# A Fourier layer and a squared-ReLU MoE on one core: a second buffer for the MoE's sums, their cast moved by a block, a fixed order of the MoE's instructions

## The chip, the core and the metric

One core of a Trainium2 chip runs the whole program. The metric is the device time of one execution in microseconds; the number given for a kernel is the median of its runs. Beside the times there is a profile of one execution, taken by the hardware profiler. In it PE is TensorE (matmuls), PEld its weight loads, DVE is VectorE, ACT ScalarE, POOL GpSimd and SP the engine that issues most DMAs. L473 is line 473 of the kernel.

## What is computed

```python
def _attn_ref(x, w_r, w_i, b_r, b_i):
    X = np.fft.rfft(x, axis=1)
    Yr = Xr @ w_r - Xi @ w_i + b_r
    Yi = Xr @ w_i + Xi @ w_r + b_i
    Yr = np.sign(Yr) * np.maximum(np.abs(Yr) - 0.01, 0.0)   # and Yi
    y = np.fft.irfft(Y, n=x.shape[1], axis=1)

def _moe_ref(x, w_in, w_out):                # 24064 x 256, 256 x 2048, 2048 x 256
    h = x @ w_in
    r = np.maximum(h, 0.0)
    return (r * r) @ w_out
```

Eight sequences of 3008 rows go through a real Fourier transform, a complex 256 x 256 mix with a bias, a soft threshold and the inverse transform. The 24,064 rows that come out go through a two-layer network of width 2048 with a squared ReLU.

## The kernel before

**Numbers in two parts.** A value in float32 is split into a high part (a cast to fp32r, on ScalarE) and a low part (value minus high part, on VectorE or GpSimd). A product takes three matmuls: high by high, low weight by high, high weight by low. The helper `halves` (L164) makes the two parts; its copy is at L89 (ScalarE) or L90 (VectorE), its subtraction at L93. These helper lines are shared by many steps, so the profile's groups are told apart by the tile that they write.

**Transforms.** The first sequence is transformed in a phase of its own (`Fwd32`, `Unit32`), together with the preparation of all weights. For the other sequences, small units of work (`Fwd`, `Pair`, `Back`) run beside the MoE of the sequence before. `Pair.load_back` (L268) loads the matrix `kcm` with a DMA that GpSimd issues. The transforms use the two PSUM banks `psf`.

**The MoE.** A sequence is cut into 6 tiles of 504 or 500 rows, so there are 48 tiles in all. Two halves of a tile's rows (`h` is 252 or 250) and two blocks of 128 hidden units make a 2 x 2 block matrix, which is multiplied with the 2 x 2 blocks of `w_out` by a scheme of seven products in place of eight (Strassen-Winograd). A *step* takes two such blocks of hidden units; a tile has 8 steps, the program 384. A step `n` consists of:

- `block(0)` and `block(1)` (L464): six matmuls each into one of two PSUM banks `psh` (L473), contraction over 256. For block 0, ScalarE writes relu to `mr` (L480) and VectorE multiplies it with max(psh, 0) into the first half of `mc` (L481). For block 1, ScalarE writes relu into the second half of `mc` (L483) and squares it in place (L484). `mc` has two buffers.
- raw parts: at the end of `block(1)`, three of the four quarters of `mc` are split into high and low parts `mb`, in two pieces, one of `h` columns and one of `2h` (L490, L491).
- sums: GpSimd makes the four sums `ms` in three instructions, one of `2h` columns (L493) and two of `h` (L494, and L495 by way of L93). `ms` has one buffer.
- `split` (L497): the four sums are split into high and low parts `mt`, `4h` columns (1008 or 1000), a ScalarE cast and a VectorE subtraction.
- `out(0)` and `out(1)` (L500): nine matmuls with the raw parts and twelve with the sums (L515), into four PSUM banks `pso` that accumulate over the tile's 8 steps. After the last step `drain` (L524) copies the banks into `me`, GpSimd makes six additions (L539), and two DMAs store the tile.

**What sets the order.** The main loop (L645) goes in half steps, `m` = 2n + k. In program order a half step holds `block(k)` of step n, at k = 0 the `split` of step n - 1, then `out(k)` of step n - 2, and then those transform jobs that are due. This order is a priority only: a planner in the compiler, which plays the program through with modelled times, puts each engine's instructions in a fixed order, and takes what it thinks ready first. `tc.issue_after` ties an instruction behind another on the same engine; before, only the first matmuls into a shared bank are tied that way. Each engine then works its list in order and waits wherever an instruction's data or buffer is not ready. Numbers of buffers stand in `MAIN` (L39); a tile not named there has two.

Of the kernel before, what the change touches and what calls it, by code (L numbers as in the profile page):

```python
# [9 lines left out]
F32 = mybir.dt.float32  # L10
# [29 lines left out]
    "xs": 1, "xe": 1, "kv": 1, "kp": 1, "kq": 1, "ksh": 1, "ksl": 1, "kxl": 1, "kb": 1, "mr": 1, "ms": 1, "me": 1,  # L40
# [10 lines left out]

A11, A12, A22, S1, S2, S3, S4 = range(7)
B11, B21, B22 = range(3)
# [4 lines left out]
def fnet_moe(ctx: ExitStack, tc, x, w_r, w_i, b_r, b_i, w_in, w_out, bm, cm, dx, a32, c32, out):  # L58
    nc = tc.nc
    act, dve, pool = nc.scalar, nc.vector, nc.gpsimd  # L60
# [31 lines left out]
    def sub(eng, out, a, b):  # L92
        return eng.tensor_tensor(out=out, in0=a, in1=b, op=ALU.subtract)  # L93
# [70 lines left out]
    def halves(hi, lo, v, eng):  # L164
        copy(act, hi, v)
        sub(eng, lo, v, hi)
# [21 lines left out]
    def wout_sums(n, pair):  # L188
        w = pair[0].wide
        a = w.rearrange("p n (f i d) -> p n f i d", f=2, i=2)  # L190
        a11, a21, a12, a22 = (a[:, :, f, i] for f in range(2) for i in range(2))
        st = T("ds", [128, 2, 4, 128], F32)
        s1, s2, s3, s4 = (st[:, :, j] for j in range(4))
        dve.tensor_add(out=s1, in0=a21, in1=a22)
        sub(dve, s2, s1, a11)
        sub(dve, s3, a11, a21)
        sub(dve, s4, a12, s2)
        hi, lo = (v[:, n:n + 2] for v in wout)
        halves(hi[:, :, A11], lo[:, :, A11], a11, dve)
        halves(hi[:, :, A12:A22 + 1], lo[:, :, A12:A22 + 1], a[:, :, 1], dve)  # L200
        halves(hi[:, :, S1:], lo[:, :, S1:], st, dve)
# [213 lines left out]
    yts = {}  # L415
# [42 lines left out]
    acc, begun = {}, {}  # L458

    class Step:  # L460
# [3 lines left out]
        def block(self, j):  # L464
# [6 lines left out]
            for c in range(2):  # L471
                for k, y in ((0, yh), (1, yh), (0, yl)):
                    nc.tensor.matmul(ps, win[k][:, c, fs], y[:, c, :w], start=n == 0, stop=n == 5)  # L473
                    n += 1
            if j == 0:
                self.c = T("mc", [128, 4 * HM], F32)[:, :2 * w]
            c = self.c[:, j * w:(j + 1) * w]
            if j == 0:
                r = T("mr", [128, 2 * HM], F32)[:, :w]
                act.activation(r, ps, AF.Relu)  # L480
                dve.scalar_tensor_tensor(out=c, in0=ps, scalar=0.0, in1=r, op0=ALU.max, op1=ALU.mult)  # L481
                return
            act.activation(c, ps, AF.Relu)  # L483
            act.activation(c, c, AF.Square)  # L484
# [8 lines left out]
            pool.tensor_tensor(out=s[:, T1:T3 + 1], in0=c[:, 1::2], in1=c[:, 0:2], op=ALU.subtract)  # L493
            pool.tensor_tensor(out=s[:, T2], in0=c[:, 0], in1=s[:, T3], op=ALU.add)  # L494
            sub(pool, s[:, T4], c[:, 2], s[:, T2])  # L495

        def split(self):  # L497
            halves(self.sum[0], self.sum[1], self.s, dve)

        def out(self, j):  # L500
            t, n, h = self.t, self.n, self.h
            if n == j == 0:
# [4 lines left out]
                ((A12, self.raw, B21, o[0], 0), (S4, self.raw, B22, o[0], 1), (A11, self.raw, B11, o[1], 0)),  # L507
# [3 lines left out]
            for a, g, b, ps, i in products:  # L511
                for k, (w, v) in enumerate(((0, 0), (1, 0), (0, 1))):
                    first = n == k == 0
                    with tc.issue_after(begun[id(ps)].ins) if first and i else nullcontext():
                        mm = nc.tensor.matmul(  # L515
                            ps[:, i], wout[w][:, n, a], g[v][:, b], start=first and i == 0,
                            stop=n == NF // 2 - 1 and k == 2 and (i == 1 or a == A22),
                        )
                    if first and not i:
                        begun[id(ps)] = mm  # L520
# [3 lines left out]
        def drain(self, j):  # L524
# [8 lines left out]
            copy(act, e[:, 4:6], o[1])  # L533
            copy(act, e[:, 6:8], o[2])
            copy(dve, e[:, 2], o[3][:, 0])
            p2, c22, p1, u2, p5, p7 = (e[:, k] for k in (0, 3, 4, 5, 6, 7))

            def add(out, a, b):
                pool.tensor_tensor(out=out, in0=a, in1=b, op=ALU.add)  # L539
# [7 lines left out]
            b, c0, _ = tiles[t]  # L547
            for d in range(2):
                nc.sync.dma_start(
                    out[b, :, d, c0:c0 + 2 * h], e[:, 2 * d:2 * d + 2].rearrange("p j h -> p (j h)")  # L550
                )
            del acc[t], yts[t]
# [91 lines left out]
    jobs = []  # L644
    for m in range(2 * len(steps) + 6):  # L645
# [111 lines left out]
```

## Time and profile before

| what | value |
|---|---|
| median of 3 runs | 2942.83 us (2940.08 to 2944.81) |
| the profiled execution's own time | 2942.48 us |
| its span, first to last instruction | 2940.7 us |
| mean granted TensorE clock | 0.966 |
| DMA, mean over the span | 85 GB/s |

The span is what the profile's rows add up to; the profiled execution takes about 2 us more than it. Busy shares are averages over the first phase, the long middle and an end with few transforms, so the prediction reads stretches apart. In the groups of instructions the columns are: line, engine, operation, output tile and input tiles, partitions x elements, count, then busy us and mean ns of one, then the engine's idle time just before them and what ended it. A row of the timeline has start, length, engine, line, operation, tiles, form, how many instructions were merged, and in brackets the idle time before and who ended it.

### The profile page before, as it was taken

The page shows a single profiled execution, that of the slowest core. Times are in us where ns is not written, and L with a number is a line of the kernel's source. Part 1 is how long each engine was busy: PE and PEld are TensorE (multiplying, and loading weights), DVE is VectorE, ACT ScalarE, POOL GpSimd, SP SyncE. Part 2 cuts the span into 40 slices and gives each one's busy share as a digit, 9 for nine tenths or more (in the row PEclk, how much of TensorE's full clock was granted, in tenths as well). Part 3 has the DMA queues.
Part 4 walks back from the last instruction along what each step waited for, and adds up shares of the span by engine and source line. Part 5 has one row for each costly group of instructions (what it writes and reads, how often), then busy time and mean ns, then how long its engine had stood idle before and what let it go on. Part 6 is the DMA issues. An engine that isn't in the chain of part 4 may idle for free.

```text
span 2940.7 us, 47049 instructions
## 1 busy us (share of the span) xinstructions
PE 2685.1 (91%) x16856; PEld 2406.9 (82%) x16856; DVE 2081.2 (71%) x3035; ACT 1789.2 (61%) x3562; POOL 2012.1 (68%) x2082
## 2 busy tenths in 40 slices
PE   5699999999999999999999999999999999998987
PEld 4588888888888898888878888888878888888877
DVE  5857876788668776678757777577775777766654
ACT  3466666666666666666656666665656665666654
POOL 3367768777776678766686667766677667666665
PEclk8899999999999999999999999999999999999998
DMA  8442324223323223322232222322233222110000
GB/s 245 154 115 87 100 82 120 84 90 97 94 80 90 78 84 106 96 81 78 63 115 84 78 83 82 104 74 80 82 92 99 72 78 85 56 35 31 24 15 15
DMA packets 191260, 250.47 MB, mean 85 GB/s; under 512 B 21755, under 2 KB 135667, under 8 KB 191027
## 3 DMA queue, kind: packets, MB, share of 16 engines
q1 hardware_dynamic: 178627, 224.85, 24.8%
q0 software_dynamic: 12400, 22.61, 3.4%
q8 instruction: 134, 2.20, 0.3%
q14 instruction: 99, 0.81, 0.1%
HBM read 146.85 MB, written 100.53 MB: 84 GB/s over the span
## 4 chain that ended last, share of the span: by engine, by line
POOL 34%; PE 30%; DVE 15%; issue 8%; ACT 7%; DMA 1%; SPq 0%; POOLq 0%; DVEq 0%; ACTq 0%
PE psh L473 14%; PE pso L515 10%; POOL ms L493 9%; POOL me L539 7%; DVE mt L93 6%; POOL ms L494 6%; POOL ms L93 6%; ACT mt L89 4%; PE psf L300 3%; POOL xs L232 3%; DVE kv L321 2%; DVE mb L93 2%; POOL ksl L93 2%; DVE mc L481 1%; POOL yt L93 1%
## 5 line engine op out<-in xcount | busy, mean ns | idle before, releaser
L473 PE MATMUL psh<-yt,win 128*128 128x500 f32 (+1 forms) x4608 | 1239.9, 404 | 93.6 <-DVE mc L481 91.8
L473 PEld LDWEIGHTS psh<-yt,win 128*128 128x128 f32 x4608 | 838.2, 194 | 246.7 <-DVE mc L481 117.8
L493 POOL TENSOR_TENSOR ms<-mc 128x500 f32<-128x500 f32 (+1 forms) x384 | 502.0, 1307 | 559.8 <-DVE mt L93 557.1
L93 DVE TENSOR_TENSOR mb<-mc,mb 128x500 fp32r<-128x500 f32 (+3 forms) x768 | 697.7, 918 | 136.2 <-ACT mb L89 132.9
L515 PEld LDWEIGHTS pso<-mt,wout 128*128 128x128 f32 x4608 | 653.6, 193 | 64.4 <-ACT mt L89 10.5
L515 PE MATMUL pso<-mt,wout 128*128 128x250 f32 (+1 forms) x4608 | 686.2, 285 | 9.9 <-ACT mt L89 8.4
L89 ACT CAST mt<-ms 128x1000 fp32r<-128x1000 f32 (+1 forms) x384 | 395.9, 1031 | 475.2 <-POOL ms L93 474.0
L93 DVE TENSOR_TENSOR mt<-ms,mt 128x1000 fp32r<-128x1000 f32 (+1 forms) x384 | 494.8, 1289 | 109.7 <-ACT mt L89 106.8
L515 PE MATMUL pso<-mb,wout 128*128 128x250 f32 (+1 forms) x3456 | 537.4, 284 | 21.2 <-DVE mb L93 21.1
L481 DVE SCALAR_TENSOR_TENSOR mc<-psh,mr 128x500 f32<-128x500 f32 (+1 forms) x384 | 260.5, 678 | 387.5 <-POOL ms L93 368.6
L515 PEld LDWEIGHTS pso<-mb,wout 128*128 128x128 f32 x3456 | 466.2, 189 | 35.1 <-DVE mb L93 26.1
L89 ACT CAST mb<-mc 128x500 fp32r<-128x500 f32 (+3 forms) x768 | 386.5, 508 | 21.4 <-DVE mc L481 8.7
L93 POOL TENSOR_TENSOR ms<-mc,ms 128x250 f32<-128x250 f32 (+1 forms) x384 | 314.4, 819 | 21.3
L494 POOL TENSOR_TENSOR ms<-mc,ms 128x250 f32<-128x250 f32 (+1 forms) x384 | 307.8, 802 | 22.0
L480 ACT ACTIVATE mr<-psh 128x500 f32<-128x500 f32 (+1 forms) x384 | 227.1, 591 | 136.0 <-PE psh L473 133.3
L539 POOL TENSOR_TENSOR me<-me 128x250 f32<-128x250 f32 (+3 forms) x288 | 288.1, 1018 | 30.0 <-ACT me L89 23.3
L484 ACT ACTIVATE mc<-mc 128x500 f32<-128x500 f32 (+1 forms) x384 | 242.1, 630 | 1.2
L483 ACT ACTIVATE mc<-psh 128x500 f32<-128x500 f32 (+1 forms) x384 | 224.5, 585 | 10.7 <-PE psh L473 10.4
L300 PE MATMUL psf<-wx,kxh 128*128 128x256 f32 x1008 | 209.4, 285 | 11.0 <-DVE kul L93 8.7
L93 POOL TENSOR_TENSOR yt<-dy,yt 128x376 fp32r<-128x376 f32 (+3 forms) x168 | 153.1, 917 | 51.2 <-ACT yt L89 46.6
L232 POOL TENSOR_TENSOR xs<-xt 120x256 f32<-120x256 f32 x182 | 164.6, 925 | 24.7 <-PE psf L235 18.1
L300 PEld LDWEIGHTS psf<-wx,kxh 128*128 128x128 f32 x1008 | 167.2, 190 | 16.2 <-DVE kul L93 12.8
(91 smaller groups left out, 2914.2 us busy)
## 6 DMA issues: line engine op xcount, KB each, us to landing
du<-s SPq DMA_DIRECT2D x128, 256.0 KB, 3.0
s<-kuh SPq DMA_DIRECT2D x192, 128.0 KB, 2.0
s<-kul SPq DMA_DIRECT2D x192, 128.0 KB, 2.5
s<-xe SPq DMA_DIRECT2D x92, 240.0 KB, 2.4
xt<-x_in SPq DMA_DIRECT2D x91, 240.0 KB, 3.1
kcm<-cm_in POOLq DMA_DIRECT2D x84, 256.0 KB, 3.5
ka<-s SPq DMA_DIRECT2D x84, 256.0 KB, 3.2
du<-s SPq DMA_DIRECT2D x256, 64.0 KB, 3.0
```

What stands on the lines that cost most here:

```text
L89: return act.copy(out=out, in_=in_)
L93: return eng.tensor_tensor(out=out, in0=a, in1=b, op=ALU.subtract)
L232: pool.tensor_tensor(out=u[:, t], in0=self.xt[:, 0, 0], in1=self.xt[:, 0, 1], op=(ALU.add, ALU.subtract)[t])
L300: self.last = nc.tensor.matmul(ps, l, wx[j][:, k, c, :], start=n == 0, stop=n == 5)
L473: nc.tensor.matmul(ps, win[k][:, c, fs], y[:, c, :w], start=n == 0, stop=n == 5)
L480: act.activation(r, ps, AF.Relu)
L481: dve.scalar_tensor_tensor(out=c, in0=ps, scalar=0.0, in1=r, op0=ALU.max, op1=ALU.mult)
L484: act.activation(c, c, AF.Square)
L493: pool.tensor_tensor(out=s[:, T1:T3 + 1], in0=c[:, 1::2], in1=c[:, 0:2], op=ALU.subtract)
L494: pool.tensor_tensor(out=s[:, T2], in0=c[:, 0], in1=s[:, T3], op=ALU.add)
L515: mm = nc.tensor.matmul(ps[:, i], wout[w][:, n, a], g[v][:, b], start=first and i == 0, stop=n == NF // 2 - 1 and k == 2 and (i == 1 or a ...
L539: pool.tensor_tensor(out=out, in0=a, in1=b, op=ALU.add)
```

## The change

- `ms` gets a second buffer. `mr` goes: the relu of block 0 is written into `mc` itself, and L481's product works in place there. `kcm` has one buffer instead of two.
- A helper `then` ties each MoE instruction behind the last one given to it on the same engine. It covers the matmuls of `block` and `out`, the relu, product and square, the three GpSimd sums, and the casts and subtractions of `mb` and `mt`. The drain's copies and additions are not tied.
- The order of a half step becomes `out(k)` of step n - 2, `block(k)` of step n, then at k = 1 the split of the sums of step n - 1 and the split of the raw parts of step n. So the cast of the sums stands behind the second block of the next step, no longer ahead of it.
- The roles of the two row halves are exchanged, so that the three raw quarters lie side by side and are split in one piece of `3h` columns (756 or 750). One sum (S3 of the weights, T3 of the activations) changes its sign, and places in `me` and the order of two products change.
- The drain's six additions and the store are taken out of `drain` into `finish`, and done one by one, one each half step, over the next seven half steps.

The core of the diff:

```diff
-    "xs": 1, "xe": 1, "kv": 1, "kp": 1, "kq": 1, "ksh": 1, "ksl": 1, "kxl": 1, "kb": 1, "mr": 1, "ms": 1, "me": 1,
+    "xs": 1, "xe": 1, "kv": 1, "kp": 1, "kq": 1, "ksh": 1, "ksl": 1, "kxl": 1, "kb": 1, "kcm": 1, "me": 1,
-B11, B21, B22 = range(3)
+B11, B22, B21 = range(3)
-        sub(dve, s3, a11, a21)
+        sub(dve, s3, a21, a11)
+    acc, last_of = {}, {}
+    def then(eng, op, *args, **kwargs):
+        with tc.issue_after(last_of[eng].ins) if eng in last_of else nullcontext():
+            last_of[eng] = op(*args, **kwargs)
+    def then_halves(hi, lo, v):
+        then(act, copy, act, hi, v)
+        then(dve, sub, dve, lo, v, hi)
...
-                    nc.tensor.matmul(ps, win[k][:, c, fs], y[:, c, :w], start=n == 0, stop=n == 5)
+                    then(pe, pe.matmul, ps, win[k][:, c, fs], y[:, c, :w], start=n == 0, stop=n == 5)
+            then(act, act.activation, c, ps, AF.Relu)
             if j == 0:
-                r = T("mr", [128, 2 * HM], F32)[:, :w]
-                act.activation(r, ps, AF.Relu)
-                dve.scalar_tensor_tensor(out=c, in0=ps, scalar=0.0, in1=r, op0=ALU.max, op1=ALU.mult)
+                then(dve, dve.scalar_tensor_tensor, out=c, in0=ps, scalar=0.0, in1=c, op0=ALU.max, op1=ALU.mult)
                 return
-            act.activation(c, ps, AF.Relu)
-            act.activation(c, c, AF.Square)
+            then(act, act.activation, c, c, AF.Square)
-            halves(self.raw[0][:, B11], self.raw[1][:, B11], c[:, 0], dve)
-            halves(self.raw[0][:, B21:], self.raw[1][:, B21:], c[:, 2:4], dve)
+            b12, b11, b22, b21 = (c[:, k] for k in range(4))
-            pool.tensor_tensor(out=s[:, T1:T3 + 1], in0=c[:, 1::2], in1=c[:, 0:2], op=ALU.subtract)
-            pool.tensor_tensor(out=s[:, T2], in0=c[:, 0], in1=s[:, T3], op=ALU.add)
-            sub(pool, s[:, T4], c[:, 2], s[:, T2])
+            then(pool, sub, pool, s[:, T1:T3 + 1], b12.unsqueeze(1).broadcast_to([128, 2, h]), c[:, 1:3])
+            then(pool, sub, pool, s[:, T2], b11, s[:, T3])
+            then(pool, sub, pool, s[:, T4], b21, s[:, T2])
         def split(self):
-            halves(self.sum[0], self.sum[1], self.s, dve)
+            then_halves(self.raw[0], self.raw[1], self.c[:, 1:])
+        def split_sums(self):
+            then_halves(self.sum[0], self.sum[1], self.s)
...
-            add(u2, u2, p1)
-            add(c22, p5, p7)
-            add(e[:, 6:8], e[:, 6:8], u2.unsqueeze(1).broadcast_to([128, 2, h]))
-            add(e[:, 0:2], e[:, 0:2], e[:, 4::2])
-            add(c22, c22, u2)
-            add(e[:, 2], e[:, 2], p7)
+        def finish(self, k):
+            if k == 6:
...
+            add = (
+                (u2, u2, p1), (c22, p5, p7), (e[:, 4:6], e[:, 4:6], u2.unsqueeze(1).broadcast_to([128, 2, h])),
+                (e[:, 0:2], e[:, 0:2], e[:, 4:8:2]), (c22, c22, u2), (c21, c21, p7),
+            )[k]
+            pool.tensor_tensor(out=add[0], in0=add[1], in1=add[2], op=ALU.add)
...
+        if 0 <= n - 2 < len(steps):
+            steps[n - 2].out(k)
         if n < len(steps):
             steps[n].block(k)
-        if k == 0 and 0 < n <= len(steps):
-            steps[n - 1].split()
-        if 0 <= n - 2 < len(steps):
-            steps[n - 2].out(k)
+        if k and 0 < n <= len(steps):
+            steps[n - 1].split_sums()
+        if k and n < len(steps):
+            steps[n].split()
+        if ends:
+            ends.pop(0)()
+        if k and n % (NF // 2) == 1 and n > 1:
+            ends += [lambda u=steps[n - 2], j=j: u.finish(j) for j in range(7)]
```

More of the change, by code (lines that the diff above doesn't have):

```diff
@@ L59, in fnet_moe @@
     nc = tc.nc
-    act, dve, pool = nc.scalar, nc.vector, nc.gpsimd
+    pe, act, dve, pool = nc.tensor, nc.scalar, nc.vector, nc.gpsimd
     w_in, w_out = w_in.bitcast(I32), w_out.bitcast(I32)
@@ L506, in out @@
             products = (
-                ((A12, self.raw, B21, o[0], 0), (S4, self.raw, B22, o[0], 1), (A11, self.raw, B11, o[1], 0)),
+                ((S4, self.raw, B22, o[0], 0), (A12, self.raw, B21, o[0], 1), (A11, self.raw, B11, o[1], 0)),
                 ((S2, self.sum, T2, o[1], 1), (S1, self.sum, T1, o[2], 0), (S3, self.sum, T3, o[2], 1),
@@ L512, in out @@
                 for k, (w, v) in enumerate(((0, 0), (1, 0), (0, 1))):
[L513 to L520, printed above, removed]
+                    then(
+                        pe, pe.matmul, ps[:, i], wout[w][:, n, a], g[v][:, b], start=n == k == i == 0,
+                        stop=n == NF // 2 - 1 and k == 2 and (i == 1 or a == A22),
+                    )
             if n == NF // 2 - 1:
@@ L643, in fnet_moe @@
         job()
-    jobs = []
-    for m in range(2 * len(steps) + 6):
+    jobs, ends = [], []
+    for m in range(2 * len(steps) + 11):
         b, r = divmod(m, slots)
```

26 lines of the change are left out of this document (13 added, 13 removed).

## The prediction

> **What bounds the kernel now.** I read the page first: busy shares and the chain that ended last.
>
> ```profile
> span 2940.7 us, 47049 instructions
> ...
> PE 2685.1 (91%) x16856; PEld 2406.9 (82%) x16856; DVE 2081.2 (71%) x3035; ACT 1789.2 (61%) x3562; POOL 2012.1 (68%) x2082
> ...
> POOL 34%; PE 30%; DVE 15%; issue 8%; ACT 7%; DMA 1%; SPq 0%; POOLq 0%; DVEq 0%; ACTq 0%
> ```
>
> TensorE is busy 91% of the span, yet GpSimd holds the largest part of the chain. So TensorE has nearly enough work to fill the time, and something on GpSimd's side breaks it up. The view of waits says what (who waited, for whom, us in total, times, longest):
>
> ```profile
> POOL ms L493 <- DVE mt L93: 557.1, 255, 4.8
> ACT mt L89 <- POOL ms L93: 474.0, 292, 5.9
> DVE mc L481 <- POOL ms L93: 368.6, 258, 6.8
> ...
> PEld psh L473 <- DVE mc L481: 117.8, 112, 4.2
> ...
> PE psh L473 <- DVE mc L481: 91.8, 81, 4.0
> POOL kul L93 <- ACT ku L89: 82.0, 20, 25.1
> ...
> POOL kcm L100 <- PE psf L332: 17.8, 17, 3.0
> ```
>
> The first two rows are a ring. GpSimd may not write the sums `ms` of a step before VectorE has split the last ones (`ms` has one buffer), and ScalarE sits at the cast `mt` until GpSimd is done. The third row is what it does to others: the product at L481 waits for GpSimd to let go of `mc`, and TensorE's next block waits for that product to empty the PSUM bank `psh`. These last rows, at most 118 us, are what reaches TensorE.
>
> Next the rate. The same two stretches, first by all engines (us, busy and instructions of PE, PEld, DVE, ACT, POOL, granted clock), then for L483 alone, which runs once a step, so that its count is the number of steps:
>
> ```profile
> 250.00:2500.00 2250.00, 2106.75 (x13551) 1901.46 (x13550) 1651.58 (x2391) 1404.39 (x2798) 1612.18 (x1673) 0.98 0.30 88
> 2650.00:2900.00 250.00, 227.35 (x1374) 203.12 (x1373) 149.94 (x190) 152.35 (x284) 160.58 (x165) 0.96 0.06 21
> ```
> ```profile
> 250.00:2500.00 2250.00, 176.51 (x302) 0.98 0.30 88
> 2650.00:2900.00 250.00, 23.34 (x40) 0.96 0.06 21
> ```
>
> While the transforms of later batches run beside the MoE, a step takes 2250/302 = 7.45 us; near the end, with hardly any transform left, 250/40 = 6.25 us. A step has 33 MoE matmuls (12 at L473, 21 at L515), so in the busy stretch there are 13551/302 - 33 = 11.9 transform matmuls beside them.
>
> The timeline of a tile's end shows the dearest single event:
>
> ```profile
> 2639.25 4.26 POOL L539 TENSOR_TENSOR me<-me 128x250 f32<-128x250 f32 x4
> ...
> 2640.27 0.59 ACT L483 ACTIVATE mc<-psh 128x504 f32<-128x504 f32 x1
> ...
> 2643.47 1.71 POOL L493 TENSOR_TENSOR ms<-mc 128x504 f32<-128x504 f32 x1
> ...
> 2645.14 1.74 POOL L539 TENSOR_TENSOR me<-me 128x500 f32<-128x500 f32 x2
> ...
> 2648.38 0.68 DVE L481 SCALAR_TENSOR_TENSOR mc<-psh,mr 128x504 f32<-128x504 f32 x1 [4.33 <-POOL ms L93]
> ...
> 2649.11 2.77 PE L473 MATMUL psh<-yt,win 128*128 128x504 f32 x6 [3.61 <-DVE mc L481]
> 2649.32 0.58 ACT L483 ACTIVATE mc<-psh 128x504 f32<-128x504 f32 x1
> ```
>
> The drain's six additions (4.26 + 1.74 us) go ahead of the sums, L481 is 4.33 us late, TensorE 3.61 us. Between the two L483 rows lie 9.05 us. And the six matmuls after the stall take 2.77 us where the next fence has 1.54: the clock was halved for a while.
>
> ```profile
> 2650.73 1.37 POOL L493 TENSOR_TENSOR ms<-mc 128x504 f32<-128x504 f32 x1 [2.38 <-DVE mt L93]
> ...
> 2651.39 1.25 DVE L93 TENSOR_TENSOR mb<-mc,mb 128x504 fp32r<-128x504 f32 x1 [0.41 <-ACT mb L89]
> ...
> 2652.18 1.05 POOL L494 TENSOR_TENSOR ms<-mc,ms 128x252 f32<-128x252 f32 x1
> ...
> 2652.85 1.54 PE L473 MATMUL psh<-yt,win 128*128 128x504 f32 x6
> 2653.31 0.73 POOL L93 TENSOR_TENSOR ms<-mc,ms 128x252 f32<-128x252 f32 x1
> ...
> 2654.23 0.86 PE L515 MATMUL pso<-mt,wout 128*128 128x252 f32 x6
> ...
> 2654.93 1.21 PE L515 MATMUL pso<-mb,wout 128*128 128x252 f32 x9
> 2655.01 0.58 ACT L483 ACTIVATE mc<-psh 128x504 f32<-128x504 f32 x1
> 2655.14 1.21 DVE L93 TENSOR_TENSOR mt<-ms,mt 128x1008 fp32r<-128x1008 f32 x1 [0.39 <-ACT mt L89]
> 2655.49 0.39 ACT L89 CAST mb<-mc 128x252 fp32r<-128x252 f32 x1
> 2655.79 0.63 ACT L484 ACTIVATE mc<-mc 128x504 f32<-128x504 f32 x1
> ...
> 2655.99 1.53 PE L473 MATMUL psh<-yt,win 128*128 128x504 f32 x6
> 2656.27 0.41 DVE L93 TENSOR_TENSOR mb<-mc,mb 128x252 fp32r<-128x252 f32 x1
> ...
> 2657.55 0.59 ACT L480 ACTIVATE mr<-psh 128x504 f32<-128x504 f32 x1 [0.49 <-PE psh L473]
> ...
> 2659.79 1.04 ACT L89 CAST mt<-ms 128x1008 fp32r<-128x1008 f32 x1 [1.65 <-POOL ms L93]
> ```
>
> A step without a drain takes 2655.01 - 2649.32 = 5.69 us here. Start to start, a block of six costs TensorE 1.38 us (2652.85 to 2654.23), six matmuls at L515 0.70 and nine 1.06, so 0.117 each. Its own need is 2 x 1.38 + 21 x 0.117 = 5.22 us a step, and 5.22 + 11.9 x 0.117 = 6.61 with the transforms, taking their matmuls at the L515 price. Against 7.45 and 6.25 that leaves 0.84 and 1.03 us a step that TensorE could win at most.
>
> **The change, part by part.** *The old ring goes.* With two buffers of `ms`, the sums of step n wait for the split of step n-2, a whole step back; the 557 us at L493 and the 474 us at ScalarE vanish as waits. The drain's additions come one per half step, so the 3.61 us stall of each tile and the slow matmuls behind it (2.77 - 1.54 = 1.2 us and more) go too: 9.05 - 5.69 = 3.4 us a tile, 48 tiles, some 160 us. What is late next is the question.
>
> *A new ring comes.* The order on ScalarE is now fixed: relu(n,1), square(n), cast of the sums of n-1, cast of the raw parts of n. On TensorE it is out(n-1,0), block(n+1,0), out(n-1,1), block(n+1,1), and out(n-1,1) needs those sums split. So from one second block to the next: block start to relu 1.56 us (2655.99 to 2657.55), relu 0.59, square 0.63, cast 1.04, less 0.09 by which one ScalarE instruction starts before the last one ends (2655.49 + 0.39 against 2655.79); 0.03 to VectorE, where the subtraction takes 1.21; 0.04 (estimate) to the third matmul of out(n-1,1), which is the first to read the low part; it and nine more, 1.17; and block(n+1,1) starts. Sum 6.18 us. TensorE reaches that third matmul by itself after 1.38 + 9 x 0.117 + 1.38 + 2 x 0.117 = 4.05 us and the data after 5.01, so it stalls some 1.0 us every step. Queued behind it there is all of its MoE order; only transform matmuls can go ahead.
>
> *The port.* A subtraction of 504 that started while GpSimd ran L493 took 1.25 us and ended 0.54 after it (2652.64 against 2652.10); undisturbed it is worth 0.68, between the 0.41 of 252 and the 1.21 of 1008. In the new order L493 of step n starts when the square ends, 2.81 us after the block's start, and with the 1.37 us of the row ends at 4.18, while the `mt` subtraction wants to start at 3.76. As in that row it then ends 0.14 us sooner than its whole length after GpSimd, at 4.18 + 1.21 - 0.14 = 5.25 instead of 4.97: 0.28 us more, loop 6.46 us. The Trainium skill, "SBUF — State Buffer", Who interferes with whom, says that a VectorE instruction with two SBUF inputs and a GpSimd one that reads SBUF exclude each other, the second waiting for the whole of the first; it speaks against this change, which puts the two on top of each other in the loop. Taken strictly it gives 5.39 and a loop of 6.60, and the gain below would be 0.14 x 376 = 53 us smaller; the row shows an overlap of 0.14 that the rule does not have.
>
> *Transforms in the loop.* ScalarE's busy time a step is 1404.39/302 = 4.65 us in the busy stretch and 152.35/40 = 3.81 at the end, so transforms bring 0.84. ScalarE's part of the loop is 2.17 of about 7 us: 31%, 0.26 us if they fall evenly; I take 0.3. Of TensorE's 1.39 us of transforms, those between the third matmul and the end of the block lengthen the loop: 2.5 of 7 us, 0.5 if evenly spread, none if all lie in the stall or before it. They are put in where the MoE matmul at hand isn't ready, so I take the middle, 0.25. VectorE may be at some transform instruction when the cast lands: 0.1, estimate. Loop with transforms: 6.46 + 0.65 = 7.11 us, above TensorE's 6.61.
>
> *Raw halves in one piece.*
>
> ```profile
> L89 ACT CAST mb<-mc 128x500 fp32r<-128x500 f32 x256 | 157.5, 615 | 2.7
> ...
> L89 ACT CAST mb<-mc 128x250 fp32r<-128x250 f32 x256 | 102.6, 401 | 10.1 <-PE pso L515 4.6 <-DVE mc L481 4.2
> ```
>
> Two casts of 615 and 401 ns become one of 750, about 0.82 us (between 615 and the 1040 of 1008): 0.2 us of ScalarE a step saved, but behind the loop's cast, so worth 0 on the path (bounds 0 and 0.2 x 384 = 77 us gained, if ScalarE were the bound; at 61% busy it isn't). The parts are needed at out(n,0), about 8.0 us after the block's start, and ready at about 6.2 to 6.9: slack of 1.1 us, which hides them; without it that wait takes the loop's place.
>
> *Small parts at nothing.* The relu into `mc` itself now waits for `mc`, but GpSimd ends the sums of n-2 some 3.2 us after their square (1.37 + 1.05 + 0.73), a step ahead. One `kcm` buffer: GpSimd's DMA issue waits for the last back matmul of the pair before, about 1.8 half steps earlier in the plan; today such waits total 17.8 us, at most 3.0 each. GpSimd's spare third covers it; behind it queue the sums. Bounds 0 and 84 x 3.0/2 = 126 us if each wait reached TensorE, of which I take none. New names of products and sign of S3: same instructions.
>
> Sum: some 320 steps with transforms (the 302 and those around that stretch) x (7.45 - 7.11) = 109 us gained; the 56 others of the 384, without, x (6.46 - 6.25) = 12 us lost. The profiled execution took 2942.48 us, 0.35 below the median of the runs, so no correction: 2942.5 - 97 = 2845 us.
>
> **The rivals.** *The cover holds.* All transform matmuls fall into the 1.0 us stall and the time before it, ScalarE's behind the casts: a step costs TensorE's 6.61, with 0.15 for jitter 6.76. 320 x 0.69 - 12 = 209 us gained, 2733 us. For it: transform jobs are listed after the MoE work of their half step. Against: in the timeline above another cast stands between L483 and L484; a ready transform copy can stand there as well.
>
> *Slower: the new ring takes more than the old one gave.* Place: ScalarE, the cast of the sums behind relu and square. If transforms fall evenly (0.35 ScalarE, 0.5 TensorE) and VectorE's subtraction stands 0.3 behind others, a step costs 6.46 + 1.15 = 7.61 us: 320 x 0.16 + 12 = 63 us lost, 3005 us. It decides from 1.0 us of transforms in the loop on. For it: at the end of the program, where nothing covers, 6.46 is over 6.25. Against: the drain's 3.4 us a tile are gone whatever happens.
>
> *Nothing moves.* The lead of the drain and the loss in the ring cancel, or the plan already had this order in substance: about 2942 us.
>
> **How the numbers follow.** Forecast 0.47, cover 0.21, slower ring 0.25, nothing 0.07. A measurement of this kernel tells about 0.2% from no change, 6 us. So faster 0.68, same 0.07, slower 0.25. The range runs from the cover's 2735 to 2985, which takes in the forecast with its bounds and the nearer half of the slower case.
>
> **What would show it.** Right: L493's wait for `mt` and ScalarE's for `ms` are nearly gone; no 3 us stall at tile ends; a new wait of TensorE at L515 for VectorE's `mt` (or ScalarE's), about 1 us, in most steps, 200 to 400 us in all; steps of about 6.5 us at the end and 7.1 before; ScalarE's order relu, square, `mt`, `mb`. Wrong: TensorE stalls at other places (psf, `mb`), or no `mt` wait at all, then the loop was miscounted; steps over 7.45 mean the third case.

## The result and the profile after

The changed kernel takes 3017.9 us (median of four runs, 3008.7 to 3021.5), the kernel before 2942.5. The ratio is 1.025 (95% interval 1.022 to 1.028): slower by 75 us, outside the forecast's range, and close to the 3005 us of the rival that ended on the slower side.

The page of the profile after, the same lines as before:

```profile
span 3019.6 us, 46324 instructions
...
PE 2707.3 (90%) x16856; PEld 2392.2 (79%) x16856; DVE 1984.2 (66%) x2651; ACT 1757.7 (58%) x3178; POOL 2277.0 (75%) x2082
...
PE 36%; DVE 19%; POOL 18%; ACT 14%; issue 6%; DMA 2%; SPq 0%; POOLq 0%; DVEq 0%; ACTq 0%
```

ScalarE and VectorE have less to do than before (one cast and one subtraction less each step), and still the time went up. GpSimd's share of the last chain fell from 34% to 18%; ScalarE's doubled to 14%, VectorE's rose to 19%. All MoE instructions now pass through one helper, so their line is L464 (casts L90, subtractions L94) and one has to go by tiles. The view of waits:

```profile
DVE mt L94 <- ACT mt L90: 710.3, 312, 6.7
ACT mc L464 <- PE psh L464: 694.7, 352, 4.6
POOL ms L94 <- ACT mc L464: 318.1, 191, 4.1
PEld pso L464 <- DVE mt L94: 223.4, 267, 2.5
PE pso L464 <- DVE mt L94: 167.5, 209, 2.3
...
ACT mt L90 <- POOL ms L94: 62.3, 38, 3.9
```

The old ring is gone: no row of GpSimd waiting for `mt`, and ScalarE's wait for the sums fell from 474 to 62 us. In its place the rows run round the other way: VectorE waits for the cast `mt`, ScalarE for TensorE's block, GpSimd for ScalarE's square, TensorE for VectorE's `mt`. Before, no TensorE wait for `mt` stood among the long ones.

The rate, from L464 on ScalarE alone in two stretches. It holds three instructions a step (two relus, one square), so the count divided by three is the number of steps:

```profile
250.00:2500.00 2250.00, 536.37 (x894) 0.98 0.29 85
2700.00:2960.00 260.00, 69.88 (x117) 0.99 0.07 21
```

That is 2250/298 = 7.55 us a step beside the transforms (before 7.45) and 260/39 = 6.67 near the end (before 6.25). And this is the new ring near the end of the program, in the timeline:

```profile
2903.22 1.51 PE L464 MATMUL psh<-yt,win 128*128 128x500 f32 x6
...
2904.77 0.59 ACT L464 ACTIVATE mc<-psh 128x500 f32<-128x500 f32 x1 [2.64 <-PE psh L464]
2905.39 0.62 ACT L464 ACTIVATE mc<-mc 128x500 f32<-128x500 f32 x1
...
2905.91 1.01 ACT L90 CAST mt<-ms 128x1000 fp32r<-128x1000 f32 x1
2906.09 1.17 POOL L94 TENSOR_TENSOR ms<-mc 128x500 f32<-128x500 f32 x1 [1.36 <-ACT mc L464]
...
2906.96 1.35 DVE L94 TENSOR_TENSOR mt<-ms,mt 128x1000 fp32r<-128x1000 f32 x1 [0.81 <-ACT mt L90]
2906.98 0.50 PE L464 MATMUL pso<-mt,wout 128*128 128x250 f32 x2
...
2908.36 1.42 PE L464 MATMUL pso<-mt,wout 128*128 128x250 f32 x10 [0.89 <-DVE mt L94]
...
2909.63 1.51 PE L464 MATMUL psh<-yt,win 128*128 128x500 f32 x6
2910.14 5.80 POOL L560 TENSOR_TENSOR me<-me 128x250 f32<-128x250 f32 x6
...
2913.37 2.00 DVE L94 TENSOR_TENSOR mt<-ms,mt 128x1000 fp32r<-128x1000 f32 x1 [2.77 <-ACT mt L90]
...
2915.42 0.85 PE L464 MATMUL pso<-mt,wout 128*128 128x250 f32 x5 [1.53 <-DVE mt L94]
```

Follow it from the top: second block at 2903.22, its relu 1.55 us later, square, cast of the sums of the step before, their subtraction, the two matmuls that need the high part alone, 0.89 us of idle TensorE, ten more matmuls, and the next second block at 2909.63. That is 6.41 us, though TensorE's work would fit into 5.2. The last lines show the other half of the story: the six additions of the drain still stand in one lump of 5.80 us. Beside them the subtraction takes 2.00 us instead of 1.35 and TensorE's stall grows to 1.53.

Where the ring comes from needs a word, because program order and the order that ran differ in the kernel before. In program order the change moves the cast of the sums from ahead of the next step's second block to behind it. In the trace before, the cast of step n already stood behind the square of step n + 1 in all of the 304 steps from the second tile to the thirty-ninth but one, in 295 of them behind the first relu of step n + 2 as well. What is new is how soon TensorE reads the result: before, the first of the twelve matmuls came after `block(0)` of step n + 3 in 259 of the 304 steps, and the last six after its `block(1)` in 272; after, all twelve come after `block(0)` of step n + 2 in every step. From the square of step n + 1 to the third of these matmuls the median is 8.0 us before and 3.6 after. So before, the chain from square to matmul reached over more than a step, and after it closes within one.

To part the ring from the additions I took the distances between one square and the next (L484 before, the second instruction of L464 above) for the 38 tiles from the second to the thirty-ninth, and averaged them by their place in the tile, in us:

```
place in the tile       1     2      3     4     5     6     7      8    mean
before               6.46  7.02  11.10  7.97  6.35  6.97  6.88   6.78   7.44
after                7.15  7.26   9.55  6.99  7.20  6.96  7.20   8.25   7.57
e4                   7.07  7.33   7.10  7.62  7.01  7.27  6.96   9.43   7.48
e2                   8.12 10.95   7.25  6.52  7.14  6.41  6.91   7.25   7.57
e3                   6.52  7.34  11.89  6.74  6.84  6.70  6.48   6.89   7.42
e6                   6.60  6.07   6.19  6.72  6.87  6.82  6.18  13.61   7.38
e7                   6.57  7.33   6.81  7.49  7.83  6.24  6.93   7.54   7.09
e9                   6.99  4.48   9.90  7.42  6.11  7.03  7.06   7.66   7.08
e12                  6.33  5.61   7.95  7.48  7.58  6.11  7.15   7.99   7.03
```

Each place is the distance from that step's square to the next one. Before, an ordinary step (all but the third and fourth) took 6.74 us, and the tile's end added 5.6. After, an ordinary step (all but the third and eighth) takes 7.13, and the tile's end adds 3.5. The change won 2.0 us a tile at the end and lost 8 x 0.38 = 3.1 in between: 1.0 us a tile, 40 us over these 38 tiles. The first tile is 6 us longer, the last 71 steps together 38, and the end behind them 4 shorter; that adds up to the 79 us between the two profiled spans.

The places don't hold the same work, so the table shows where time passes and not yet what costs it. Before, TensorE has 19.6 transform matmuls in the third place and 8.6 to 13.5 in the others; after, 14.0 in the third, 12.9 in the eighth and 9.6 to 12.3 elsewhere. TensorE's idle time tells the same story in smaller numbers: before, 2.7 us in the third and fourth place together and 0.2 in each of the others, 3.9 a tile; after, 2.3 in the third and eighth together and 0.4 in each of the others, 4.6 a tile.

The ring of the changed kernel can be taken apart in every step, from the first matmul of a second block to that of the next one. Mean us: 41 ordinary steps near the end (the 329th to the 382nd), and of the 38 tiles above the 228 ordinary steps, the third and the eighth:

```
piece                                   near the end  ordinary  third  eighth
second block to its relu                        1.59      1.65   1.75    1.64
relu to square                                  0.63      0.72   0.67    0.74
square to the cast of the sums                  0.53      0.57   2.51    0.59
the cast                                        1.02      1.02   1.03    1.02
its end to the subtraction                      0.03      0.14   0.28    0.09
the subtraction                                 1.44      1.54   1.45    1.50
its end to the third matmul                     0.06      0.29   0.13    1.40
third matmul to the next second block           1.26      1.24   1.51    1.25
sum                                             6.56      7.17   9.32    8.23
```

Near the end the third matmul starts within 0.1 us of the subtraction's end in all 41 steps, beside the transforms in 69% of the ordinary ones: there the ring sets the step, though transform matmuls fill most of TensorE's stall. In the third step the cast is 2.0 us late, because it waits for sums that stand behind the additions. In the eighth the sums are ready, and TensorE comes 1.1 us later to them, because transform matmuls stand ahead in its order.

### The profile page after: what moved, and what is told of

Its sections match the earlier page's. It is cut to its first block, busy times and chain, and to the rows that moved or that the text cites. A ratio compares the mean times of both kernels' runs of the same rounds, so it can differ in the third digit from the quotient of the medians.

```text
span 3019.6 us, 46324 instructions
## 1 busy us (share of the span) xinstructions
PE 2707.3 (90%) x16856; PEld 2392.2 (79%) x16856; DVE 1984.2 (66%) x2651; ACT 1757.7 (58%) x3178; POOL 2277.0 (75%) x2082
## 4 chain that ended last, share of the span: by engine, by line
PE 36%; DVE 19%; POOL 18%; ACT 14%; issue 6%; DMA 2%; SPq 0%; POOLq 0%; DVEq 0%; ACTq 0%
PE pso L464 15%; PE psh L464 15%; DVE mt L94 10%; POOL ms L94 7%; ACT mt L90 6%; ACT mc L464 5%; POOL me L560 5%; POOL xs L233 4%; PE psf L301 4%; DVE kv L322 3%; DVE mb L94 2%; DMA du<-s 1%; POOL yt L94 1%; PE psf L236 1%; DVE mc L464 1%
## 5 line engine op out<-in xcount | busy, mean ns | idle before, releaser
L464 PE MATMUL psh<-yt,win 128*128 128x500 f32 (+1 forms) x4608 | 1211.6, 396 | 1.4 <-DVE mc L464 1.2
L94 DVE TENSOR_TENSOR mt<-ms,mt 128x1000 fp32r<-128x1000 f32 (+1 forms) x384 | 579.1, 1508 | 711.1 <-ACT mt L90 710.3
L464 PEld LDWEIGHTS psh<-yt,win 128*128 128x128 f32 x4608 | 825.3, 191 | 125.1 <-DVE mc L464 2.0
L94 POOL TENSOR_TENSOR ms<-mc,ms 128x250 f32<-128x250 f32 (+1 forms) x768 | 875.7, 1140 | 46.5
L464 PE MATMUL pso<-mt,wout 128*128 128x250 f32 (+1 forms) x4608 | 711.6, 293 | 193.6 <-DVE mt L94 167.5
L464 ACT ACTIVATE mc<-psh 128x500 f32<-128x500 f32 (+1 forms) x768 | 451.9, 588 | 697.3 <-PE psh L464 694.7
L464 PEld LDWEIGHTS pso<-mt,wout 128*128 128x128 f32 x4608 | 607.3, 192 | 282.8 <-DVE mt L94 223.4
L94 POOL TENSOR_TENSOR ms<-mc 128x500 f32<-128x500 f32 (+1 forms) x384 | 503.8, 1312 | 330.4 <-ACT mc L464 318.1
L94 DVE TENSOR_TENSOR mb<-mc,mb 128x750 fp32r<-128x750 f32 (+1 forms) x384 | 540.6, 1408 | 3.2 <-ACT mb L90 2.5
L464 PE MATMUL pso<-mb,wout 128*128 128x250 f32 (+1 forms) x3456 | 501.6, 283 | 1.7 <-DVE mb L94 1.7
L464 PEld LDWEIGHTS pso<-mb,wout 128*128 128x128 f32 x3456 | 473.8, 190 | 34.1 <-DVE mb L94 1.9
L90 ACT CAST mt<-ms 128x1000 fp32r<-128x1000 f32 (+1 forms) x384 | 391.6, 1020 | 62.6 <-POOL ms L94 62.3
L90 ACT CAST mb<-mc 128x750 fp32r<-128x750 f32 (+1 forms) x384 | 314.4, 819 | 0.0
L464 DVE SCALAR_TENSOR_TENSOR mc<-psh,mc 128x500 f32<-128x500 f32 (+1 forms) x384 | 256.5, 668 | 12.7 <-ACT mc L464 11.1
L464 ACT ACTIVATE mc<-mc 128x500 f32<-128x500 f32 (+1 forms) x384 | 239.8, 625 | 9.2
L94 POOL TENSOR_TENSOR yt<-dy,yt 128x376 fp32r<-128x376 f32 (+3 forms) x168 | 149.9, 894 | 114.6 <-ACT yt L90 113.7
L90 ACT CAST yt<-dy 128x376 fp32r<-128x376 f32 (+3 forms) x168 | 71.8, 432 | 192.9 <-DVE dy L446 119.9
L322 DVE TENSOR_TENSOR kv<-psf,ke 64x256 f32<-64x256 f32 x336 | 141.2, 420 | 46.2 <-PE psf L301 41.9
```

The lines of the kernel that those rows point to most:

```text
L90: return act.copy(out=out, in_=in_)
L322: dve.tensor_add(out=v[64 * r:64 * r + 64, g], in0=ps[gs], in1=self.e[gs, r])
L464: last_of[eng] = op(*args, **kwargs)
```

## The experiments

The theory after the result: the fixed order closes a loop through ScalarE (second block, relu, square, cast of the sums of the step before, subtraction, the matmuls that use them, next second block), and this loop sets the step. The rivals: the ties cost as such, because the planner can't fill holes; the additions' lump on GpSimd; the single `kcm` buffer or the one-piece split.

**e1: lengthen the loop by a known piece.**

```diff
-        if k and 0 < n <= len(steps):
-            steps[n - 1].split_sums()
         if k and n < len(steps):
             steps[n].split()
+        if k and 0 < n <= len(steps):
+            steps[n - 1].split_sums()
```

> The changed kernel, with the cast and subtraction of the raw parts put ahead of those of the sums. Same work, same ties. Theory (a loop through block(n,1), relu, square, cast of the sums of n-1, their subtraction, out(n-1,1), block(n+1,1) sets the step): the loop gets the raw cast's 0.82 less 0.10 us and some 0.2 to 0.4 us of waiting behind the raw subtraction, 0.7 to 1.1 us a step, 384 steps: 3290 to 3440 us. Rivals (the ties as such, the six additions still in a lump, or the single kcm buffer set the time): about 3018 us, within 1%.

Measured: 3553.3 us, ratio to before 1.208 (1.206 to 1.210). The same instructions in the same number, two of them exchanged, cost 535 us over the changed kernel, 1.39 us a step. The loop in the timeline:

```profile
3440.40 0.50 PE L464 MATMUL pso<-mt,wout 128*128 128x250 f32 x2 [0.71 <-ACT mt L90]
...
3442.29 1.76 PE L464 MATMUL pso<-mt,wout 128*128 128x250 f32 x10 [1.40 <-DVE mt L94]
...
3443.85 2.71 PE L464 MATMUL psh<-yt,win 128*128 128x500 f32 x6
...
3447.21 0.62 ACT L464 ACTIVATE mc<-mc 128x500 f32<-128x500 f32 x1
...
3447.87 0.82 ACT L90 CAST mb<-mc 128x750 fp32r<-128x750 f32 x1
...
3448.59 1.02 ACT L90 CAST mt<-ms 128x1000 fp32r<-128x1000 f32 x1
3448.72 1.17 DVE L94 TENSOR_TENSOR mb<-mc,mb 128x750 fp32r<-128x750 f32 x1 [5.89 <-ACT mb L90]
...
3449.81 1.71 DVE L94 TENSOR_TENSOR mt<-ms,mt 128x1000 fp32r<-128x1000 f32 x1
...
3451.58 0.62 PE L464 MATMUL pso<-mt,wout 128*128 128x250 f32 x3 [1.41 <-DVE mt L94]
```

From the square's start to the third matmul are 4.37 us here, against 2.97 in the ring above (2905.39 to 2908.36): 1.40 us, the measured 1.39 of a step. The rivals foresaw no change. The loop sets the step. It was dearer than the expected 0.7 to 1.1 us: the subtraction of the sums waits longer behind the raw one on VectorE (0.61 us from the cast's end in ordinary steps, against 0.14), and the clock dropped (below).

**e2: open the loop at the cast.**

```diff
-        if k and 0 < n <= len(steps):
+        if k == 0 and 0 < n <= len(steps):
             steps[n - 1].split_sums()
```

> The changed kernel, with the split of the sums of step n-1 moved back half a step: behind block(n,0), ahead of the second relu of step n. All ties stay. Theory (the loop): the cast no longer waits for the relu and the square of the next second block, so the loop is open; TensorE's own 6.6 us with transforms plus some jitter: 2760 to 2860 us, and TensorE's 390 us of waits for VectorE's mt vanish. Rival (the ties as such cost, because the planner can't fill holes): 2980 to 3030 us. Rival (the old ring of before comes back): about 2940 us.

Measured: 2993.2 us, ratio 1.018 (1.016 to 1.019). The theory as it stood fell short by 130 us. (Its 390 us of waits add up those of the weight loads and of the matmuls, which run side by side; the matmuls' own are 167.5.) Near the end of the program the step did come down, to 5.63 us in the middle of a tile (fourth to sixth step, tiles 43 to 47) from 6.47; but with the additions in a lump, the second step of a tile takes 10.95 us. The view of waits shows a second wait behind the first: ScalarE now waits 559 us for the sums (62 in the changed kernel), and when GpSimd is at the additions, that wait holds the relus queued behind it.

```profile
ACT mt L90 <- POOL ms L94: 558.7, 290, 6.4
```

**e3: ties on TensorE alone.**

```diff
-        with tc.issue_after(last_of[eng].ins) if eng in last_of else nullcontext():
+        with tc.issue_after(last_of[eng].ins) if eng in last_of and eng is pe else nullcontext():
```

> The changed kernel with the ties kept on TensorE alone; ScalarE, VectorE and GpSimd are ordered by the planner. Theory (the loop): the planner lets the sums' cast go ahead of the second relu when its data are ready, so this opens the loop as well: 2760 to 2900 us. Rival (the ties as such): the same, so this run alone doesn't part the two. Rival (one kcm buffer, raw parts in one piece): no better than 2980 us.

Measured: 2957.7 us, ratio 1.005 (1.004 to 1.007). Ordinary steps fell to 6.5 to 6.9 us, as they should with the loop open, but the third step of a tile grew to 11.89, more than before the change. So it misses the expected 2760 to 2900. The additions still stand in lumps here as in e2, and TensorE is idle for 3.0 us of the third step, 1.6 of them for `mt`; that the lump is the whole reason is not shown.

**e4: spread the additions.** In `finish`, the addition goes through `then(pool, ...)`.

> The changed kernel with the drain's six additions tied into GpSimd's order too, so that they come one per half step as the text of the change has it. Theory (the loop): only the waits of ScalarE for the sums, 62 us in all, can go, and part of the VectorE subtraction's blocking: 2950 to 3010 us. Rival (the lump of additions at the tile's end sets the time): 48 tiles x some 3.4 us, 2850 us or less.

Measured: 2989.2 us, ratio 1.016 (1.015 to 1.018), 29 us below the changed kernel and inside the loop's 2950 to 3010. The third step falls from 9.55 to 7.10 us, the lump is off it, but the eighth grows from 8.25 to 9.43, and ordinary steps stay at 7.0 to 7.6: the ring is still there. In the eighth step the third matmul starts 2.55 us after the subtraction's end, where the ring near the end has 0.06: TensorE has 14.7 transform matmuls in this place, against 8.9 to 13.1 in the others. The lump by itself is not the cause.

**e5 and e6: cut the ring at TensorE.** The swap alone, and with the additions tied as in e4.

```diff
-        if 0 <= n - 2 < len(steps):
+        if k == 0 and 0 <= n - 2 < len(steps):
             steps[n - 2].out(k)
         if n < len(steps):
             steps[n].block(k)
+        if k and 0 <= n - 2 < len(steps):
+            steps[n - 2].out(k)
```

> The changed kernel with one swap on TensorE: at k = 1, block(n,1) stands ahead of out(n-2,1), not behind it. Casts, buffers and ties stay. Theory (the loop): the next second block no longer waits for the sums of the step before, so the loop is cut at its other end; the sums are needed 1.4 us later, about when they are ready. Steps of some 5.6 us without transforms and 6.8 to 7.1 with: 2740 to 2860 us, TensorE's waits for mt under 100 us. A stall of 1 to 2 us may come at tile ends, where out of the new tile needs the bank that was just finished. Rival (GpSimd's work and its port set the step, since GpSimd's transforms stand among the sums): 2950 us or more, with TensorE waiting for mc or mb in place of mt.

> As e5_block_before_out, with the six additions tied in GpSimd's order as in e4_additions_tied. Theory (the loop): 10 to 40 us below e5_block_before_out. Rival (GpSimd): 100 us below it.

Measured: 2902.8 us, ratio 0.987 (0.984 to 0.989), and 2885.0 us, ratio 0.981 (0.979 to 0.983). One swap takes 115 us off the changed kernel, and TensorE's wait for `mt` falls from 167.5 to 33.8 us. e6 is 18 us below e5, as the loop had it. In e6, near the end, TensorE runs without a hole:

```profile
2799.82 2.66 PE L464 MATMUL psh<-yt,win 128*128 128x500 f32 x11
...
2802.32 1.54 PE L464 MATMUL pso<-mt,wout 128*128 128x250 f32 x12
...
2803.70 1.22 PE L464 MATMUL pso<-mb,wout 128*128 128x250 f32 x9
...
2804.76 2.88 PE L464 MATMUL psh<-yt,win 128*128 128x500 f32 x12
```

Two blocks, the twelve and the nine matmuls, and the next blocks 4.94 us later, with one matmul of the first row missing from the trace and no idle time before any row. Yet both times lie above the 2740 to 2860 expected of e5: the eighth step of a tile takes 12.88 us in e5 and 13.61 in e6. In e6 24.6 transform matmuls stand in this place, against 5.8 to 12.7 in the others, and TensorE is idle for 3.0 us among them, waiting for other engines; some of these transforms make the rows of the next tile. Why the planner piles them up there was not tried.

**e7: both at once, early cast and spread additions.**

> e2_sums_cast_early with the six additions tied in GpSimd's order. In e2 the cast of the sums stands ahead of the second relu, and ScalarE waits 559 us for GpSimd there. If it is a second loop, through GpSimd (relu, square, three sums with transforms among them, cast, next relu), then spreading the lump helps at tile ends only: 2930 to 2975 us. If the lump alone held e2 back: 2850 us or less.

Measured: 2829.3 us, ratio 0.962 (0.960 to 0.964): 164 us below e2, where 20 to 60 were expected from the ring through GpSimd and more from the lump. So the lump was the larger part of what held e2 back. TensorE's wait for `mt` in e2 and then in e7:

```profile
PE pso L464 <- DVE mt L94: 117.8, 133, 4.2
```
```profile
PE pso L464 <- DVE mt L94: 59.8, 91, 4.6
```

With e2 and e4 this makes a square: late cast 3018, with spread additions 2989; early cast 2993, with spread additions 2829. Either repair alone is worth 25 to 29 us, both are worth 189. Two waits stand behind each other, and opening one leaves the other.

**e8: the buffers alone.** The kernel before with two `ms` buffers, one `kcm`, the relu of block 0 into `mc`:

```diff
-    ... "kb": 1, "mr": 1, "ms": 1, "me": 1,
+    ... "kb": 1, "kcm": 1, "me": 1,
-                r = T("mr", [128, 2 * HM], F32)[:, :w]
-                act.activation(r, ps, AF.Relu)
-                dve.scalar_tensor_tensor(out=c, in0=ps, scalar=0.0, in1=r, op0=ALU.max, op1=ALU.mult)
+                act.activation(c, ps, AF.Relu)
+                dve.scalar_tensor_tensor(out=c, in0=ps, scalar=0.0, in1=c, op0=ALU.max, op1=ALU.mult)
```

> The kernel before with the buffers of the change alone: two for ms, one for kcm, the relu of block 0 written into mc. Order, casts in two pieces, the lump of additions as before. Theory (the old ring cost about 0.2 to 0.5 us a step, the new ring took it back): 2850 to 2930 us, GpSimd's wait at L493 for mt gone. Rival (the old ring cost nothing beyond the tile ends): 2940 us, no change.

Measured: 2835.0 us, ratio 0.964 (0.962 to 0.966), a little better than expected. GpSimd's first wait is now for its data, no longer for its buffer:

```profile
POOL ms L492 <- ACT mc L483: 290.0, 166, 4.5
```

The buffers of the change are worth 105 us by themselves. The single `kcm` buffer is in this kernel, so it isn't what made the change slow. The run doesn't part the three buffers from each other.

**e9: the whole change without its ties.** Only the first matmul into a shared bank stays tied, as before.

```diff
-        with tc.issue_after(last_of[eng].ins) if eng in last_of else nullcontext():
-            last_of[eng] = op(*args, **kwargs)
+        last_of[eng] = op(*args, **kwargs)
```

> The changed kernel without its ties, but for those that put the first matmul into a shared bank first, as before. Buffers, one-piece raw halves and the half step's new program order stay. If the ties are what costs (they make the loop, and e8_before_two_ms_buffers without them took 2835): 2830 to 2890 us. If TensorE's order, free here and tied in e3_ties_on_pe_alone (2958), doesn't matter: about 2958. If the one-piece split or the single kcm buffer costs: 2940 us or more.

Measured: 2810.7 us, ratio 0.956 (0.954 to 0.958). The one-piece split and the program order with the late cast are in it, and it is faster than e8 and below the 2830 to 2890 that were expected if the ties cost. So the ties in this order cost 207 us against the changed kernel. How the planner can use its freedom shows on ScalarE:

```profile
2708.64 1.03 ACT L90 CAST mt<-ms 128x1000 fp32r<-128x1000 f32 x1 [1.49 <-POOL ms L94]
...
2709.57 1.06 ACT L463 ACTIVATE mc<-psh 128x500 f32<-128x500 f32 x2
2710.66 0.62 ACT L463 ACTIVATE mc<-mc 128x500 f32<-128x500 f32 x1
```

Here the cast of the sums stands ahead of both relus and the square of a step. That is one place of several: of the 304 steps counted above, the cast of step n has the square of step n + 1 ahead of it in 105, where the changed kernel has it so in all.

**e10: e8 with the additions one each half step**, GpSimd's sums and additions tied in that order.

> e8_before_two_ms_buffers, with the six additions taken out of the drain, one each half step, and GpSimd's sums and additions alone tied in that order. Spreading the lump took 164 us from e2 to e7, where ScalarE waits for the sums. Here the planner orders ScalarE, which waits 308 us for GpSimd. If the lump still costs about 3.4 us at each of 48 tile ends: 2680 to 2760 us. If two buffers already hide it: 2820 to 2840 us.

Measured: 2808.2 us, ratio 0.955 (0.953 to 0.957), 27 us below e8: below the 2820 to 2840 of "two buffers already hide it" and far above the other range. The lump is worth little there.

**e11: e7 with ties on TensorE and GpSimd alone.**

> e7_sums_early_tied with ties on TensorE and GpSimd alone; ScalarE and VectorE are the planner's. If their ties cost where the sums are cast early: 2760 to 2810 us. If they don't: 2820 to 2840 us. If GpSimd's transforms set the step in both: no change.

Measured: 2846.1 us, ratio 0.968 (0.965 to 0.970), 17 us above e7 and 6 above the range for "they don't". Where the order is a good one, ties on ScalarE and VectorE don't cost; the planner did slightly worse. That speaks against ties as such.

**e12: e9 with GpSimd's ties alone**, so that the additions come one by one and everything else is the planner's.

> e9_no_ties with GpSimd's sums and additions tied in the program's order, so that the additions come one by one; TensorE, ScalarE and VectorE stay the planner's. In e9 the third step of a tile is still the longest. If the lump is what is left at the tile's end: 2740 to 2800 us. If spreading only moves the wait to the end of the tile, as from e8 to e10 (27 us gained): 2780 to 2815 us.

Measured: 2789.5 us, ratio 0.949 (0.947 to 0.950), the fastest of all, 228 us below the changed kernel. It lies in both expected ranges, so it doesn't part them; the table shows the third step falling from 9.90 to 7.95 us while the second, fifth and eighth grow. The same count of steps as for the changed kernel, in e12:

```profile
250.00:2500.00 2250.00, 578.08 (x967) 1.00 0.31 90
```

967/3 = 322 steps, 6.99 us each, at a granted clock of 1.00. TensorE's own need was put at 6.61.

## Why the prediction was wrong

**The new ring, right, its sum in part by luck.** The prediction added it up to 6.46 us, 1.0 us of stall in it; the trace has 6.41 and 0.89. Two misses cancel there: the subtraction takes 1.35 us, where 1.21 and 0.28 of blocking were priced, and from the third matmul to the next block it is 1.27, where 1.17 was priced. The form of the blocking was right: GpSimd's sum ends at 2907.26 and the subtraction 1.05 us later, less than its undisturbed 1.19, so the stricter reading, a loop of 6.60, isn't what the trace shows. Its size came out at half because that sum takes 1.17 us in the ring and not 1.37. The sign that was named, a wait of about 1 us for `mt` in most steps, 200 to 400 us in all, is weaker: 209 waits of the matmuls, 167.5 us. Beside the transforms other matmuls fill the stall, and the step still ends with the ring. e1 lengthens this ring, e5 cuts it, e9 lets it go, and the time follows.

**Transforms in the ring, right in sum.** 7.11 us a step were forecast, and ordinary steps took 7.13. Of the 0.65 us put in for transforms, 0.61 came (7.17 less 6.56), otherwise spread: ScalarE 0.13 where 0.3 was taken, TensorE 0.23 where 0.25 was, VectorE 0.21 where 0.1 was, and 0.06 ahead of the relu.

**The step that failed: "The drain's additions come one per half step, so the 3.61 us stall of each tile and the slow matmuls behind it (...) go too".** They don't come one per half step. `finish` is called so, but the additions are not tied; the program's order is a priority, and the planner took them together. The trace has four or six additions without a sum between them at 45 of the first 47 tile ends. The third step of a tile takes 9.55 us and the eighth 8.25, 3.5 us a tile over the ordinary step. The forecast applied 7.11 to every step and so put the tile's end at nothing, while the 7.45 that it subtracted from held the old tile ends; 40 tiles x 3.5 us are 142 us, and near the end 56 x (6.67 - 6.46) are 12 more. 2845 + 154 = 2999, against 3018 measured; the other 19 us are not assigned. Only the third step's part is the additions. And e4 shows that spreading them would not have saved the forecast: it is worth 29 us, the ring remains, and TensorE's transforms make the tile's last step longer.

A slip of the sum beside it: 320 and 56 steps are 376 of the 384. The other 8 are worth 3 us at most at either price.

**The old ring goes, right.** Its first row is gone and its second fell to 62 us, and e8 puts the worth of the buffers at 105 us. The forecast of 2845 us comes close to what the buffers do alone (2835), but by another road.

**The slower rival, right in total, half right in cause.** It named the place, ScalarE's cast behind relu and square, and 7.61 us a step; 7.55 was measured. It got there by transforms falling evenly into the ring, which ordinary steps of 7.13 don't bear out. The rest is the tile's end, so that its total fits is luck in this part. "It decides from 1.0 us of transforms in the loop on" was the wrong point; with 0.61 us of transforms in the ring it was the tile ends that decided.

**The cover, wrong.** With the ring cut (e6) TensorE runs full near the end, but steps beside transforms average 7.38 us: the transforms don't slip into holes freely, they pile up in the tile's last step.

**Small parts at nothing.** The one-piece split cost nothing that e9 shows, and TensorE waited for the raw parts once, 1.7 us; the single `kcm` buffer raised GpSimd's wait for back matmuls from 17.8 to 27.1 us in total, while e8 and e9, which have it too, gain.

Open: why the planner puts more transforms into the eighth step of a tile when the others shrink, and how much of e3's loss is the lump (its third step is 11.89 us) and how much TensorE's fixed order otherwise. e11 has the same TensorE ties with spread additions and an early cast, and is 112 us faster, but it differs in two things.

## What to carry to other kernels

A buffer that opens one ring is worth only what the next ring leaves, so add up the loop that the new order closes, engine by engine, before fixing the order by hand: here TensorE was made to read the sums one step after a cast that stands right behind relu and square, a loop of 6.4 us around 5.2 us of matmuls. Compare with the order that ran, not with the program's order: the kernel before had the cast behind these two as well and gave the chain a step more. In this kernel it paid to fix the order where the planner did harm (GpSimd's lump: e9 to e12, 21 us) and to leave it free elsewhere. And work that is meant to be spread must be tied to be spread; calling it later in the program only lowers its priority.

## What the runs showed of the hardware

The granted clock fell after shorter stalls than the 3.61 us that the prediction showed. In e1, idle times of 0.71 and 1.40 us within 2 us (3440.40 and 3442.29 above) were followed by a block of six matmuls in 2.71 us instead of 1.52, at a granted clock of 0.50 from 3443.8 to 3446.6 us; the mean clock of that run was 0.935. One stall of 0.89 us a step did not do it: the changed kernel has 0.99 from 2700 to 2960 us. Over the whole span it has 0.976 against 0.966 before, so the clock is not what made it slower.

The subtraction `mt` took 1.35 us beside one GpSimd sum and 2.00 us beside the additions, with 1.19 undisturbed. What decides is how much of GpSimd's instruction is left: of the 384 subtractions in the changed kernel, 332 began at least 0.1 us after a GpSimd instruction did and with more than 0.15 us of it to come, and every one of them ended 1.05 to 1.08 us after that instruction's end. So in these two instructions VectorE did all but some 0.13 us of its work after GpSimd was done.
